# Attention, experts and MLP on one core: score matmuls of two key blocks in the two halves of TensorE's rows, scores computed three steps ahead, gate and float64 splits moved into the expert stage

## The chip, the core and the metric

The program runs on one core of a Trainium2 chip, as one launch. The metric is the device time in microseconds (us). TensorE (PE) multiplies, VectorE (DVE) and ScalarE (ACT) do the element-wise work, GpSimd (POOL) does some of it and issues the indirect transfers, SyncE (SP) issues the other transfers. PE writes only to PSUM, which has eight banks of 2 KB in each of 128 partitions.

## The reference

Three layers follow each other on 24,576 tokens (8 batches of 3,072) of width 256:

```python
# attention: z is (8, 3072, 64), u and v are (8, 3072, 256)
attn = np.maximum((1.0 / S) * z @ z.transpose(0, 2, 1), 0.0) ** 2
x = (u * (attn @ v)).reshape(B * S, D)
# mixture of 8 experts, one for each token
logits = normalise(x) @ normalise(expert_emb).T / tau
idx = argmax(logits, axis=1); gate = softmax(logits)[token, idx]
out[mask_e] = gate * (np.maximum(x[mask_e] @ w1[e], 0.0) @ w2[e])   # w1 256x1024, w2 1024x256
# MLP; w_in (256x2048) and w_out (2048x256) arrive as float64
h = out @ w_in; y = (h - np.tanh(h)) @ w_out
```

## The kernel before, in words

Every float32 operand of a matmul is kept as two parts, a rounded high part and the remainder (`split`, line 102), and a product is made of three matmuls: high by high, high by low, low by high.

**Attention.** A batch has 3,072 keys in 24 blocks of 128. The queries are taken 512 at a time (a *query block*; 48 in all, numbered q), and for each of them the keys two blocks at a time: 12 *steps* per query block, 576 in all, numbered G.

`emit_S(G)` (line 486) makes the scores of step G. z has 64 columns, so a transposed tile `zt` holds the high part of z in partitions 0 to 63 and the low part in 64 to 127; `zs` is the same with the halves swapped, made by two DMAs (`z_swap`). One matmul of `zt` by `zt` over all 128 rows gives high by high plus low by low, and one of `zt` by `zs` gives the two mixed products: two matmuls of 512 columns for a key block, four in a step (lines 493, 494), into a two-bank PSUM tile `s`. Then ACT takes relu (line 500) and square (501), ACT or DVE rounds the square to `ah` (502, the choice is `on_act`), and DVE subtracts to get the remainder `al` (503).

`emit_AV(G)` (line 505) multiplies by v: 24 matmuls of 256 columns (lines 519, 520, 521: `ah` by `vh`, `ah` by `vl`, `al` by `vh`) into `acc`, two banks for a query block. The loop at the end of `attention` issues `emit_S(step + 2)`, `emit_AV(step)` and then whatever the table `steps` holds for this step, so scores are two steps ahead, and the ACT and DVE work on them is issued together with them. All engines take their instructions in this order.

After the last step of a query block, `r_x` (537) multiplies `acc` by u on DVE, into rows `xr`. In the steps that follow come the routing: row norms (`r_n`, ACT), 32 products with the expert embeddings (`r_l`, line 555, DVE), softmax and first maximum (`r_s1`, `r_s2`), ranks by a small matmul (`r_pe`, copied out of PSUM by ACT), the gate times the rows (`r_g`, line 266, DVE), positions (`r_s3`) and a scatter to DRAM (`r_sc`, POOL). In the same stage the expert weights are split (`w_split`: ACT, POOL, and back to DRAM), and w_in and w_out are converted from float64 and split (`f64_split`: nine DVE operations at line 590 and three on POOL for each of 16 pieces) and stored in DRAM.

In PSUM, attention has four single-bank accumulators (two query blocks) and two two-bank score tiles, which the transposes of z and the ranks use as well.

**Experts.** 100 tiles of 256 tokens: `gather` (POOL, indirect), `trans` (PE transposes, line 309, and a split), `up` and `down` (three matmuls a product again). Five gather buffers. Six transfers (`w_piece`) bring the split w_in and half of w_out from DRAM.

**MLP.** 512 tokens at a time against all of w_in and w_out, which lie in SBUF; the change touches only where these weights come from.

Of the kernel before, what the change touches and what calls it, by code (L numbers as in the profile page):

```python
# [12 lines left out]
I32 = mybir.dt.int32  # L13
# [11 lines left out]
def tile_attention_moe_mlp(  # L25
# [31 lines left out]
    ROW = D + 1  # L57
# [7 lines left out]
    wsi = dram.tile([P, 2, KD * F2], F32, tag="wsi", name="wsi")  # L65
    wso = dram.tile([P, 2, KF2 * D], F32, tag="wso", name="wso")
# [162 lines left out]
    def r_s1(q):  # L229
# [13 lines left out]
        nc.vector.tensor_tensor(out=oh, in0=w, in1=b3(m8), op=ALU.is_equal)  # L243
        r["ex"] = ex = sm.tile([P, 4, E], F32, tag="ex", name=f"ex{q}")
        nc.scalar.activation(out=ex, in_=lg, func=AF.Exp)

    def r_s2(q):
# [10 lines left out]
        nc.vector.reciprocal(sx, sx)  # L258
        r["gate"] = sx

    def r_g(q):
        r = RT[q]
        for j in range(4):
            sx = r["gate"]
            x = r["xr"][:, j, 0:D]
            nc.vector.tensor_scalar(out=x, in0=x, scalar1=sx[:, j:j + 1], scalar2=None, op0=ALU.mult)

    def r_pe(q):
        r = RT[q]
        rp = ps_s(f"rp{q}", (P, 2, 256))  # L270
        rp = rp[:, 0, 0:4 * E].rearrange("p (j e) -> p j e", j=4)
        nc.tensor.matmul(rp, tri, r["oh"], start=True, stop=False)
        nc.tensor.matmul(rp, ones, r["cp"], start=False, stop=True)
        r["rk"] = rk = sm.tile([P, 4, E], F32, tag="rk", name=f"rk{q}")
        nc.scalar.copy(rk, rp)
# [28 lines left out]

    def trans(t):
        pt = ps_a(f"xt{t}", (P, KD * TT))
# [8 lines left out]
    def attention(L1, R1, RE):  # L315
# [3 lines left out]
        pr = pool(L1, "pr", 2)  # L319
        pa = pool(L1, "pa", 3)  # L320
        pzs = pool(L1, "pzs", 3)
        pzt = pool(L1, "pzt", NCH + 2)
        pvh = pool(L1, "pvh", NPR + 2)
# [3 lines left out]
        pc = pool(R1, "pc", 1, "right")  # L327
# [4 lines left out]
        ZR, ZZ, ZT, ZS, VR, VH, VL = {}, {}, {}, {}, {}, {}, {}  # L332
# [10 lines left out]
        def z_first():  # L343
            zr = ZR.pop((0, 0))
            ZZ[0, 0] = t = pz.tile([P, 4, P], FR, tag="zz", name="zz0_0")
            w = pz.tile([P, 4, P], FR, tag="zw", name="zw", bufs=1)
            split(t[:, :, 0:64], t[:, :, 64:P], zr, copy=nc.vector.tensor_copy)
            split(w[:, :, 64:P], w[:, :, 0:64], zr)
            z_trans(0, 0)
            z_split(0, 1, nc.vector.tensor_copy)  # L350
# [6 lines left out]
        def z_trans(b, c):  # L357
            zz = ZZ.pop((b, c))
            pt = ps_s(f"pt{b}_{c}")
            for j in range(4):  # L360
                nc.tensor.transpose(pt[:, 0, j * P:(j + 1) * P].bitcast(FR), zz[:, j, :], identr)
            ZT[b, c] = t = pzt.tile([P, 512], FR, tag="zt", name=f"zt{b}_{c}")
            nc.scalar.copy(t, pt[:, 0, :])
# [11 lines left out]
        def v_split(b, g, cp=None):  # L375
            VH[b, g] = h = pvh.tile([P, 2, D], FR, tag="vh", name=f"vh{b}_{g}")
            VL[b, g] = l = pvh.tile([P, 2, D], FR, tag="vl", name=f"vl{b}_{g}")
            cp = cp or (nc.vector.tensor_copy if on_act(g - 2) else nc.scalar.copy)
# [102 lines left out]
        AH, AL, ACC = {}, {}, {}  # L481

        def on_act(step):
            return 2 <= step % NPR < 10 or step // NPR == NQ - 1

        def emit_S(G):
            q, g = divmod(G, NPR)
            b, c = divmod(q, NCH)
            sp = ps_s(f"s{G}")
            for i in range(2):  # L490
                kb = 2 * g + i
                zt = ZT[b, kb // 4][:, (kb % 4) * P:(kb % 4 + 1) * P]
                nc.tensor.matmul(sp[:, i, :], zt, ZT[b, c], start=True, stop=False)
                nc.tensor.matmul(sp[:, i, :], zt, ZS[b, c], start=False, stop=True)  # L494
            r = pr.tile([P, 2, 512], F32, tag="r", name=f"r{G}")
            a = pr.tile([P, 2, 512], F32, tag="a", name=f"a{G}")
            AH[G] = h = pa.tile([P, 2, 512], FR, tag="ah", name=f"ah{G}")
            AL[G] = l = pa.tile([P, 2, 512], FR, tag="al", name=f"al{G}")
            for i in (slice(0, 1), slice(1, 2)) if G == 0 else (slice(0, 2),):
# [77 lines left out]
        def idle():  # L577
            pass
# [501 lines left out]
```

## Time and profile before

| what | us |
|---|---|
| median of 3 runs (5693.11 to 5703.36) | 5699.75 |
| profiled execution, device time | 5693.57 |
| its span | 5692.0 |
| attention, from the start to the last product with v (2296.6) | 2297 |
| experts, to the last product of `down` (3503.5) | 1207 |
| MLP, to the end | 2188 |

Over the span PE is busy 5600.8 us (98%), DVE 4597.2 (81%), ACT 3704.8 (65%), POOL 2054.1 (36%). A matmul's busy time runs from its first column to its last result, so that the bars of matmuls that follow each other overlap; the spacing of their starts tells what one costs. PEld is the loading of a matmul's stationary operand; it is shown apart, and a wait of a matmul often stands there. A wait that ends at an engine which is not the bottleneck costs nothing by itself. The granted clock of TensorE is 0.998 of full speed over the run, that is its higher level, 2.4 GHz.

### The profile page before, as it was taken

Reading aid. Unit: us, or ns where it says so; the run is one execution under the profiler, and the core shown is the slowest. Engines: PE = TensorE matmul, PEld = TensorE weight load, DVE = VectorE, ACT = ScalarE, POOL = GpSimd, SP = SyncE. Lnnn points to the kernel's source line nnn. Section 1 sums busy time; section 2 is a strip of 40 time slices with the busy share of each in tenths; the row PEclk is TensorE's granted clock in tenths of the full one; section 3 lists DMA queues with packets and bytes.
Section 4 is the critical chain, followed back from the end, with each engine's and each line's share of the span. In section 5 each row is a group of like instructions: output and inputs, shape, how many; then the busy total and the mean of one; then the engine's idle time right before and its main releaser. Section 6 shows DMA issues by size and latency. Waiting matters only on the chain. (4 is left out here: it accounts for less than half of the span.)

```text
span 5692.0 us, 99647 instructions
## 1 busy us (share of the span) xinstructions
PE 5600.8 (98%) x38768; PEld 5202.0 (91%) x38768; DVE 4597.2 (81%) x7691; ACT 3704.8 (65%) x4509; POOL 2054.1 (36%) x1381
## 2 busy tenths in 40 slices
PE   9999999999999999999999999999999999999999
PEld 9999999999999999999999998999999999999998
DVE  7989988888989887633333335999999999999999
ACT  8778777777777777322222224777777777777776
POOL 2323232222322221322222221555555555555554
PEclk9999999999999999999999999999999999999999
DMA  2222222222222111344443441000000000000000
GB/s 77 89 73 86 69 87 76 83 72 82 79 80 75 58 41 40 86 117 106 103 105 103 117 127 53 23 23 23 26 26 24 24 23 23 23 28 24 25 23 19
DMA packets 178733, 347.44 MB, mean 61 GB/s; under 512 B 49745, under 2 KB 90194, under 8 KB 173010
## 3 DMA queue, kind: packets, MB, share of 16 engines
q1 hardware_dynamic: 147026, 264.14, 15.9%
q0 software_dynamic: 31232, 76.89, 4.4%
q8 instruction: 307, 5.03, 0.4%
q14 instruction: 168, 1.38, 0.1%
HBM read 520.29 MB, written 118.69 MB: 112 GB/s over the span
## 5 line engine op out<-in xcount | busy, mean ns | idle before, releaser
L521 PE MATMUL acc<-vh,al 128*128 128x256 f32 x4608 | 1308.6, 284 | 38.3 <-DVE al L503 35.2
L519 PE MATMUL acc<-vh,ah 128*128 128x256 f32 x4608 | 1302.3, 283 | 4.3 <-DVE ah L502 4.3
L520 PE MATMUL acc<-vl,ah 128*128 128x256 f32 x4608 | 1302.2, 283 | 0.0
L104 POOL TENSOR_TENSOR gl<-gg,gh 128x1024 fp32r<-128x1024 f32 x381 | 915.1, 2402 | 1009.9 <-ACT gh L103 1003.5
L521 PEld LDWEIGHTS acc<-vh,al 128*128 128x128 f32 x4608 | 879.8, 191 | 51.0 <-DVE al L503 51.0
L519 PEld LDWEIGHTS acc<-vh,ah 128*128 128x128 f32 x4608 | 878.4, 191 | 31.8 <-DVE ah L502 8.6
L520 PEld LDWEIGHTS acc<-vl,ah 128*128 128x128 f32 x4608 | 879.9, 191 | 25.1
L503 DVE TENSOR_TENSOR al<-a,ah 128x1024 fp32r<-128x1024 f32 (+1 forms) x577 | 757.8, 1313 | 141.9 <-ACT ah L502 122.7
L995 PE MATMUL mo<-wo,gl 128*128 128x256 f32 x3072 | 869.5, 283 | 0.0
L993 PE MATMUL mo<-wo,gh 128*128 128x256 f32 x3072 | 868.5, 283 | 0.0
L994 PE MATMUL mo<-wo,gh 128*128 128x256 f32 x3072 | 866.8, 282 | 0.0
L957 ACT ACTIVATE ga<-mh 128x1024 f32<-128x1024 f32 x384 | 395.2, 1029 | 547.2 <-PE mh L955 542.7
L555 DVE CUSTOM_DVE_ANT_0 jl<-xr,en 128x256 f32<-128x256 f32 x1504 | 711.0, 473 | 39.1
L965 DVE TENSOR_SCALAR gm<-ga 128x1024 int32<-128x1024 f32 x384 | 733.2, 1909 | 0.0
L500 ACT ACTIVATE r<-s 128x1024 f32<-128x1024 f32 (+1 forms) x577 | 588.8, 1021 | 216.1 <-PE s L494 211.2
L501 ACT ACTIVATE a<-r 128x1024 f32<-128x1024 f32 (+1 forms) x577 | 611.6, 1060 | 18.3
L953 PE MATMUL mh<-yh,wi 128*128 128x512 f32 (+1 forms) x1568 | 610.4, 389 | 7.9 <-DVE gg L963 6.2
L955 PE MATMUL mh<-yh,wi 128*128 128x512 f32 (+1 forms) x1568 | 611.3, 390 | 0.0
L954 PE MATMUL mh<-yl,wi 128*128 128x512 f32 (+1 forms) x1568 | 610.3, 389 | 0.0
L814 PE MATMUL y<-hh,w 128*128 128x512 f32 x1600 | 581.0, 405 | 18.0 <-DMA w<-ws 15.6
L993 PEld LDWEIGHTS mo<-wo,gh 128*128 128x128 f32 x3072 | 583.6, 190 | 16.4
L994 PEld LDWEIGHTS mo<-wo,gh 128*128 128x128 f32 x3072 | 583.8, 190 | 15.8
(196 smaller groups left out, 12514.6 us busy)
## 6 DMA issues: line engine op xcount, KB each, us to landing
w<-ws SPq DMA_DIRECT2D x180, 2048.0 KB
ys<-yo SPq DMA_DIRECT2D x100, 256.0 KB
vr<-in_v_dram SPq DMA_DIRECT2D x96, 256.0 KB
u<-in_u_dram SPq DMA_DIRECT2D x48, 512.0 KB
yr<-ys SPq DMA_DIRECT2D x47, 512.0 KB
wr<-in_moe_w_dram SPq DMA_DIRECT2D x64, 256.0 KB
ws<-wh SPq DMA_DIRECT2D x64, 256.0 KB
ws<-wl SPq DMA_DIRECT2D x64, 256.0 KB
```

Of the source, the lines that this page charges most:

```text
L104: (eng or nc.vector).tensor_tensor(out=lo, in0=src, in1=hi.bitcast(F32), op=ALU.subtract)
L501: nc.scalar.activation(out=a[:, i], in_=r[:, i], func=AF.Square)
L503: nc.vector.tensor_tensor(out=l[:, i], in0=a[:, i], in1=h[:, i].bitcast(F32), op=ALU.subtract)
L519: nc.tensor.matmul(o, h[:, i, js], vh[:, i, :], start=first, stop=False, skip_group_check=True)
L520: nc.tensor.matmul(o, h[:, i, js], vl[:, i, :], start=False, stop=False, skip_group_check=True)
L521: nc.tensor.matmul(o, l[:, i, js], vh[:, i, :], start=False, stop=last, skip_group_check=True)
L555: nc.vector.tensor_tensor_reduce(out=jk, in0=r["xr"][:, j, 0:D], in1=en[:, e, :], scale=1.0, scalar=0.0, op0=ALU.mult, op1=ALU.add, accum_ ...
L955: nc.tensor.matmul(pv[:, i, :], wi[:, 1, k, fs], yh[:, k, :], start=False, stop=k == KD - 1)
L965: nc.vector.tensor_scalar(out=m, in0=a, scalar1=THR, scalar2=None, op0=ALU.is_gt)
L993: nc.tensor.matmul(o, h[:, i, js], wo[:, 0, fo, :], start=first, stop=False, skip_group_check=True)
L994: nc.tensor.matmul(o, h[:, i, js], wo[:, 1, fo, :], start=False, stop=False, skip_group_check=True)
L995: nc.tensor.matmul(o, l[:, i, js], wo[:, 0, fo, :], start=False, stop=last, skip_group_check=True)
```

## The change

1. **Scores.** A key block's score is now three matmuls over 64 rows (high by high, high by low, low by high; the product of the two low parts is left out). The first key block of a step uses partitions 0 to 63, the second 64 to 127, in turn, so that two matmuls that follow each other lie in different halves of the rows and write different PSUM banks. `zs` is now needed for the keys too.
2. **Order.** Scores are made for three steps at once (18 matmuls), three steps before they are used. Relu, square and split are no longer issued with them but spread over the following three steps (`cycle`). `r_x` is issued ahead of the other element-wise work of its step.
3. **PSUM.** Three two-bank score tiles and one pair of accumulators instead of two and two. The ranks are read from PSUM by DVE (`r_s3`), without the copy; the transposes of z are copied out a step later (`z_copy`).
4. **Casts.** Of every four `ah`, three are made on ACT and one on DVE (before: by `on_act`, 386 and 191). The v splits alternate between the two.
5. **Gate.** The gate is written as one more column of the scattered row (`ROW = D + 2`), and applied after the gather (`scale`, two DVE operations for a tile) instead of before the scatter.
6. **float64.** The 16 pieces are converted in the expert stage, three parts of a piece for each tile, straight into the MLP's tiles; only the second half of w_out goes through DRAM.
7. `r_l` uses `scalar_tensor_tensor` in place of `tensor_tensor_reduce`.

```diff
+        def emit_S(G):
+            SP[G] = sp = ps_s(f"s{G}")
+            TS = ZT, ZS
+            for ki, qi in ((0, 0), (0, 1), (1, 0)):
+                for i in range(2):
+                    kb = 2 * g + i
+                    h = slice(64 * i, 64 * i + 64)
+                    zk, zq = TS[ki ^ i][b, kb // 4], TS[qi ^ i][b, c]
+                    nc.tensor.matmul(sp[:, i, :], zk[h, (kb % 4) * P:(kb % 4 + 1) * P], zq[h, :],
+                                     start=ki == qi, stop=ki == 1)
+        def emit_R(G, i=slice(0, 2)):
...
+            nc.scalar.activation(out=RS[G][:, i], in_=SP[G][:, i], func=AF.Relu, scale=1.0 / S)
+        def emit_A(G, i=slice(0, 2)):
...
+            nc.scalar.activation(out=a, in_=a, func=AF.Square)
+            split(AH[G][:, i], AL[G][:, i], a, copy=nc.vector.tensor_copy if G % 4 == 3 or G == 0 else None)
...
+        cycle = ["r0 r1 a0", "r2 a1", "a2"]
         for step in range(-2, NG):
-            if step + 2 < NG:
-                emit_S(step + 2)
+            base = step - step % GS + GS
+            scores, after = plan.get(step) or (range(base, base + GS) if step == base - GS else (), cycle[step % GS])
+            for G in scores:
+                if G < NG:
+                    emit_S(G)
             if step >= 0:
                 emit_AV(step)
+            # r_x of this step, then the parts named in `after`, then the rest of the step's table
...
+    def scale(t):
+        for j in range(JT):
+            x = XG[t][:, j, 0:D]
+            nc.vector.tensor_scalar(out=x, in0=x, scalar1=XG[t][:, j, D + 1:D + 2], scalar2=None, op0=ALU.mult)
...
@@ experts: each(t)
-            if t in pieces:
-                w_piece(pieces.index(t))
+            if t > K0 and (parts or todo):
+                bg_step()
+                bg_step()
+                bg_step()
...
-                PS["a"] = pool(L1, "psA", 4, space=PSUM)
-                PS["s"] = pool(L1, "psS", 2, space=PSUM)
+                PS["a"] = pool(L1, "psA", 2, space=PSUM)
+                PS["s"] = pool(L1, "psS", 3, space=PSUM)
```

How the order moves, at three places. First PE at the end of query block 16 and the start of block 17 (`acc16`, `acc17` are their accumulators, `s206` a score tile by its step number, `zt2_5` the tile of batch 2 and key group 5). Before:

```order
L521 MATMUL acc16_1_10218<-vh2_11_7656,al203_10683 128x256
L361 MATMUL pt3_0_10825<-identr_75,zz3_0_10712 128x128 x4
L493 MATMUL s206_10849<-zt2_5_7654,zt2_1_7173 128x512
L494 MATMUL s206_10849<-zs2_5_9634,zt2_1_7173 128x512
L493 MATMUL s206_10849<-zt2_5_7654,zt2_1_7173 128x512
L494 MATMUL s206_10849<-zs2_5_9634,zt2_1_7173 128x512
L519 MATMUL acc17_0_10862<-vh2_0_6983,ah204_10736 128x256
```

The same place now, up to the second of three score tiles:

```order
L533 MATMUL acc16_1_10205<-vh2_11_7823,al203_10631 128x256
L501 MATMUL s207_10812<-zt2_5_7589,zt2_1_7150 128x512
L501 MATMUL s207_10812<-zs2_5_7591,zs2_1_7152 128x512
L501 MATMUL s207_10812<-zs2_5_7591,zt2_1_7150 128x512
L501 MATMUL s207_10812<-zt2_5_7589,zs2_1_7152 128x512 x2
L501 MATMUL s207_10812<-zs2_5_7591,zt2_1_7150 128x512
L501 MATMUL s208_10819<-zt2_5_7589,zt2_2_7345 128x512
L501 MATMUL s208_10819<-zs2_5_7591,zs2_2_7347 128x512
```

Steps 207, 208 and 209 now stand together, 18 score matmuls, between the last product into `acc16` and the first into `acc17` (which is now the same pair of banks); where one step's four stood, and none stands before the next two steps.

Second DVE at the same place; `xr16` is `r_x` of block 16, which reads the accumulators. Before:

```order
L502 CAST ah205_10795<-a205_10794 128x1024
L503 TENSOR_TENSOR al205_10796<-a205_10794,ah205_10795 128x1024
L104 TENSOR_TENSOR zz3_1_10832<-zr3_1_10653,zz3_1_10832 128x4x64
L537 TENSOR_TENSOR xr16_10841<-acc16_0_10217,u16_10258 128x2x256
L537 TENSOR_TENSOR xr16_10841<-acc16_1_10218,u16_10258 128x2x256
L502 CAST ah206_10856<-a206_10855 128x1024
L503 TENSOR_TENSOR al206_10857<-a206_10855,ah206_10856 128x1024
L266 TENSOR_SCALAR xr15_10196<-xr15_10196,sx15_10780 128x256 x4
```

Third DVE a little later, in the third step of the next block, now (`rp16` is the tile of the ranks in PSUM, `jl17` the scratch of `r_l`):

```order
L103 TENSOR_TENSOR al220_11630<-a220_11580,ah220_11629 128x1024
L567 SCALAR_TENSOR_TENSOR jl17_0_0_11641,lg17_11592<-xr17_11508,en_157 128x256
L567 SCALAR_TENSOR_TENSOR jl17_0_1_11643,lg17_11592<-xr17_11508,en_157 128x256
L567 SCALAR_TENSOR_TENSOR jl17_0_2_11645,lg17_11592<-xr17_11508,en_157 128x256
L567 SCALAR_TENSOR_TENSOR jl17_0_3_11647,lg17_11592<-xr17_11508,en_157 128x256
L103 TENSOR_TENSOR al221_11674<-a221_11627,ah221_11673 128x1024
L278 TENSOR_TENSOR t16_11678<-rp16_11634,ecap_86 128x32
L279 TENSOR_TENSOR t16_11678<-t16_11678,oh16_11443 128x32
```

The row with `rp16` frees a score tile's place in PSUM and stands behind the remainder `al221` of the last of the three steps; before, ACT's copy of the ranks freed it in the step in which they were made, and the multiplication by the gate (line 266) is gone from this queue.

## Rows read from the trace of the kernel before

**Rows 1.** Busy time by stretch: start, end, its length, each engine's busy time

```profile
0.00:20.00 20.00, 14.50 (x86) 12.60 (x87) 13.42 (x29) 13.36 (x19) 5.73 (x12) 1.00 0.49 151
20.00:2290.00 2270.00, 2219.04 (x16282) 2098.66 (x16281) 1984.22 (x5283) 1772.27 (x2196) 606.06 (x489) 1.00 0.22 72
2290.00:3490.00 1200.00, 1182.03 (x8413) 1106.83 (x8412) 441.49 (x790) 348.28 (x611) 286.66 (x308) 0.99 0.41 105
3490.00:5692.00 2202.00, 2185.25 (x13992) 1983.87 (x13990) 2158.02 (x1591) 1570.92 (x1686) 1155.61 (x573) 1.00 0.08 25
```

**Rows 2.** Waits of PE's weight loads, 0 to 2290: total, times, longest

```profile
PEld acc L521 <- DVE al L503: 51.0, 63, 2.0
...
PEld s L493 <- ACT r L500: 11.3, 14, 1.8
...
PEld acc L519 <- DVE ah L502: 8.6, 10, 1.1
```

**Rows 3.** Timeline of PE, one step: start, duration, line

```profile
1002.97 0.40 PE L493 MATMUL s<-zt,zt 128*128 128x512 f32 x1
...
1003.90 0.28 PE L519 MATMUL acc<-vh,ah 128*128 128x256 f32 x1
1004.02 0.28 PE L520 MATMUL acc<-vl,ah 128*128 128x256 f32 x1
...
1006.76 0.40 PE L493 MATMUL s<-zt,zt 128*128 128x512 f32 x1
```

**Rows 4.** Timeline around one wait for a remainder; brackets: idle before, releaser

```profile
2008.69 0.28 PE L519 MATMUL acc<-vh,ah 128*128 128x256 f32 x1
2008.69 0.19 PEld L520 LDWEIGHTS acc<-vl,ah 128*128 128x128 f32 x1
...
2009.22 0.19 PEld L521 LDWEIGHTS acc<-vh,al 128*128 128x128 f32 x1 [0.34 <-DVE al L503]
2009.22 0.39 PE L521 MATMUL acc<-vh,al 128*128 128x256 f32 x1
```

**Rows 5.** ACT's groups, 0 to 2290: count, busy, mean ns, idle before

```profile
L501 ACT ACTIVATE a<-r 128x1024 f32<-128x1024 f32 x575 | 610.4, 1062 | 18.2
L500 ACT ACTIVATE r<-s 128x1024 f32<-128x1024 f32 x575 | 587.7, 1022 | 214.8 <-PE s L494 209.8 <-issue 2.4
L502 ACT CAST ah<-a 128x1024 fp32r<-128x1024 f32 x386 | 406.2, 1052 | 12.2
L548 ACT ACTIVATE jk<-xr 128x256 f32<-128x256 f32 x188 | 78.1, 415 | 35.6 <-DVE xr L537 32.7
...
L548 ACT ACTIVATION_READ_ACCUMULATOR jk<-xr 128x1 f32 x188 | 35.2, 187 | 0.0
```

**Rows 6.** DVE's groups, 0 to 2290

```profile
L503 DVE TENSOR_TENSOR al<-a,ah 128x1024 fp32r<-128x1024 f32 x574 | 755.2, 1316 | 141.5 <-ACT ah L502 122.4 <-DVE ah L502 1.4 <-issue 0.8
L555 DVE CUSTOM_DVE_ANT_0 jl<-xr,en 128x256 f32<-128x256 f32 x1504 | 711.0, 473 | 39.1
...
L502 DVE CAST ah<-a 128x1024 fp32r<-128x1024 f32 x189 | 129.7, 686 | 81.3 <-ACT a L501 76.4 <-PE acc L521 4.9
...
L266 DVE TENSOR_SCALAR xr<-xr,sx 128x256 f32<-128x256 f32 x184 | 85.7, 527 | 0.0
L537 DVE TENSOR_TENSOR xr<-acc,u 128x512 f32<-128x512 f32 x94 | 60.2, 683 | 0.0
...
L590 DVE TENSOR_SCALAR qe<-qr 128x512 int32<-128x512 int32 x32 | 13.5, 421 | 0.0
...
L590 DVE SCALAR_TENSOR_TENSOR qm<-qe,qp 128x512 f32<-128x512 int32 x16 | 11.0, 687 | 0.0
```

**Rows 7.** Waits in the expert stage, 2290 to 3490

```profile
POOL xg L300 <- PE xt L309: 692.3, 86, 10.6
...
PE y L814 <- DMA w<-ws: 15.6, 9, 4.2
```

**Rows 8.** One line's instructions: the products with `al`, first and last start

```profile
L521 PE MATMUL acc<-vh,al x4608: 277/283/436, 12.8 to 2296.6; 128*128 128x256 f32 x192
```

More of the change, by code (lines that the diff above doesn't have):

```diff
@@ L257, in r_s2 @@
         nc.vector.tensor_scalar(out=sx, in0=sx, scalar1=1e-9, scalar2=None, op0=ALU.add)
[L258 to L266, printed above, removed]
+        nc.vector.reciprocal(r["xr"][:, :, D + 1:D + 2], sx[:, :, None])
     def r_pe(q):
@@ L488, in emit_S @@
             b, c = divmod(q, NCH)
[L489 to L499, printed above, removed]
-                nc.scalar.activation(out=r[:, i], in_=sp[:, i], func=AF.Relu, scale=1.0 / S)
-                nc.scalar.activation(out=a[:, i], in_=r[:, i], func=AF.Square)
-                (nc.scalar.copy if on_act(G - 2) else nc.vector.tensor_copy)(h[:, i], a[:, i])
-                nc.vector.tensor_tensor(out=l[:, i], in0=a[:, i], in1=h[:, i].bitcast(F32), op=ALU.subtract)
+            SP[G] = sp = ps_s(f"s{G}")
[8 more added lines that the diff above has]
+        def emit_R(G, i=slice(0, 2)):
+            if G not in RS:
+                RS[G] = pr.tile([P, 2, 512], F32, tag="a", name=f"a{G}")
+            nc.scalar.activation(out=RS[G][:, i], in_=SP[G][:, i], func=AF.Relu, scale=1.0 / S)
+        def emit_A(G, i=slice(0, 2)):
+            if G not in AH:
+                AH[G] = pa.tile([P, 2, 512], FR, tag="ah", name=f"ah{G}")
+                AL[G] = pa.tile([P, 2, 512], FR, tag="al", name=f"al{G}")
+            a = RS[G][:, i]
+            nc.scalar.activation(out=a, in_=a, func=AF.Square)
+            split(AH[G][:, i], AL[G][:, i], a, copy=nc.vector.tensor_copy if G % 4 == 3 or G == 0 else None)
         def emit_AV(G):
@@ L554, in r_l @@
                 jk = pj.tile([P, D], F32, tag="junk2", name=f"jl{q}_{e}_{j}")
[L555 to L557 removed]
+                nc.vector.scalar_tensor_tensor(
+                    out=jk, in0=r["xr"][:, j, 0:D], scalar=1.0, in1=en[:, e, :],
+                    op0=ALU.mult, op1=ALU.mult, accum_out=r["lg"][:, j, e:e + 1])
         bg = []
@@ new lines, in jobs @@
+        def jobs():
+            a = w_out.bitcast(I32).rearrange("(k p) f -> p k f", p=P)
+            kk = CW // D
+            half = KF2 // 2 // kk
+            WO0 = WO[0].rearrange("p a k f -> p a (k f)")
+            for k in [*range(half, 2 * half), *range(half)]:
+                yield a[:, k * kk:(k + 1) * kk, :], wso if k >= half else WO0, k % half * CW
+            a = w_in.bitcast(I32).rearrange("(k p) f -> p k f", p=P)
+            WI0 = WI[0].rearrange("p a k f -> p a (k f)")
+            for k in range(KD):
+                for f in range(F2 // CW):
+                    yield a[:, k:k + 1, 2 * f * CW:2 * (f + 1) * CW], WI0, k * F2 + f * CW
@@ L779, in weights, with bg_step @@
+        todo, parts = list(jobs()), []
+        def bg_step():
+            if not parts and todo:
+                parts.extend(f64_split(*todo.pop(0), len(todo)))
+            if parts:
+                parts.pop(0)()
         def weights(t, W, ws):
@@ L855, in run @@
             tokens(t0 + 1)
+            scale(t0 + 2)
             each(-1)
@@ L882, in each @@
                 y_load(1)
-        pieces = [NT0 - 8 - max(1, NT0 // 24) * i for i in range(6)][::-1]
         run(0, NT0, each)
+        assert not parts and not todo
         if NT0 < NT:
```

259 lines of the change are left out of this document (130 added, 129 removed).

## The prediction

> **What bounds the kernel now.** I read the busy time by stretch first. PE is busy 2219 of 2270 us in attention, 1182 of 1200 in the experts, 2185 of 2202 in the MLP [rows 1]: the end is set by PE throughout, and a change pays by what it takes from PE's stream or from its waits. The MLP keeps its instructions, so attention and experts are left.
>
> Next the timeline of PE, for the price of a matmul by spacing. One step is 1002.97 to 1006.76, 3.79 us: four score matmuls in 0.93 us (0.2325 each), then 24 products with v in 2.86 us (0.119 each) [rows 3]. 576 steps of 3.79 are 2183 us, and the stage's last product starts at 2296.6 [rows 8].
>
> Then PE's waits. Most are for the remainder `al`, 51.0 us in 63 waits; for `ah` 8.6; and 11.3 before the scores, for the relu that frees a score tile [rows 2]. That is 71 us, in a stage where DVE works 1998 us and ACT 1786 of 2290 [rows 1]: neither is full, they are late.
>
> **Scores.** Before, 4 matmuls a step, 12 in three steps: 12 x 0.2325 = 2.79 us. Now 18 matmuls of 512 columns over 64 rows, in nine pairs in different halves. No row shows two halves working at once. The bounds: a pair costs what one matmul costs (9 x 0.2325 = 2.09 us), or the halves take turns (18 x 0.2325 = 4.19). I take 2.09: the columns of a pair go to different rows and different banks, and weights already load while a matmul runs: the load for L520 starts at 2008.69, the instant at which L519 starts [rows 4]. Two loads for a pair must fit into 0.2325; a load that nothing hides lengthens a product by 0.11 (0.39 against 0.28) [rows 3, 4], so two are 0.22, which fits barely. Gain: 0.70 us x 192 triples = 134 us.
>
> **Turning between whole and half rows.** Twice in a triple PE goes from 128-row matmuls to 64-row ones and back. A product's bar is 0.28 us at a spacing of 0.119 [rows 3], so 0.16 us pass between its last column and its last result. If PE runs empty at each turn, that is 2 x 0.16 x 192 = 61 us. Bounds: nothing, or 0.27 a turn (0.16 and an unhidden load of 0.11) and 0.12 once for the second half starting late, 0.66 x 192 = 127 us. I take 61.
>
> The Trainium skill, "TensorEngine Tiling (Array Packing)", section "Key Properties", says that a change of tiling mode drains TensorE; it speaks against this change and prices nothing. No run here shows a turn yet. By that rule the sum holds the 61 us above; without it they would be gone and the time 61 us lower.
>
> **Waits removed.** Relu, square and split of a triple are issued over the three steps before its first product. ACT's work for a triple is 3 x 1.02 + 3 x 1.06 + 2.25 x 1.05 = 8.6 us [rows 5]; the first `al` is ready some 5 us into the triple and wanted 11 us in, at the next triple's products. So the 60 us of waits for `al` and `ah` go. The 11 us before the scores I leave in. Bounds 0 and 71.
>
> Does ACT or DVE become late as a whole? Casts on ACT go from 386 to 432 (+48 us), the v splits add about 11, the copies of ranks go (-9): 1786 + 50 = 1836 us, 9.6 for a triple. DVE loses the float64 work (16 pieces, five operations of 421 and four of about 687 ns, 78 us), the gate (86) and 46 casts of 686 ns (32) [rows 6]: 1998 - 196 = 1802, 9.4. PE's triple is 3 x 2.86 + 2.09 + 0.32 = 11.0 us. Both fit, with little over. I count nothing for `scalar_tensor_tensor` in `r_l`: it would come off an engine that has room (nearest row 473 ns for 256 elements; were it slower by a third, DVE would have 1.2 us more a triple, 10.6, and still fit).
>
> **Waits added.** (a) The ranks hold a score tile until DVE has read them behind `al` of the triple's last step. In the block's first triple ACT starts when the first tile is there (0.16 + 0.70 = 0.9 us), then has 8.3 us (one cast on DVE) and four row norms of 0.6 [rows 5], so it ends at 11.6 us; `al` takes 1.3 [rows 6], 12.9. PE wants that place for the third tile of the next triple at 11.0 + 0.16 + 1.4 = 12.6. Behind that matmul stands PE's whole stream. With half a weight split (0.3) on ACT the wait is some 0.5 us, in 46 blocks 23 us; bounds 0 and 60 (1.3 each). (b) One pair of accumulators: `r_x` (2 x 0.683 us [rows 6]) must end before the next block's products, behind a burst of 2.1 us or more. The first half is needed first, so 1.4 us of cover remain against a DVE operation under way; I count 0.1 x 47 = 5 us, bounds 0 and 0.68 x 47 = 32 (no cover).
>
> **Experts.** DVE gets 200 `scale` operations (527 ns, 106 us) and the 78 us of float64: 441 + 184 = 625 of 1200 us [rows 1, 6], and does not bound. `scale(t + 3)` waits for a gather, and the next tile's split, which PE wants, stands behind it in DVE's queue. But POOL waits 692 us for the transposes that free a gather buffer [rows 7]: gathers already run as far ahead as five buffers allow. On POOL the three float64 operations of a piece wait for DVE and hold the gathers behind them for about one tile of 12 us (1200 us for 100); three tiles of lead cover that. On SP, 16 loads and 8 stores wait likewise and hold the weight loads, for which PE waits 15.6 us now [rows 7]. I take 0, bounds -10 and +16 (the same again). The longer row (two columns) adds nothing to a stream at 22% of the DMA engines [rows 1].
>
> **Sum.** -134 + 61 - 60 + 23 + 5 = -105 us. The profiled execution took 5693.6 us (span 5692.0), so 5589; the median of the runs is 6 us above that execution, so I forecast 5595 us.
>
> **Rivals.**
>
> *Turns are free.* For: no row shows PE emptying between unlike matmuls. Against: a product's result stands 0.16 us behind its last column [rows 3], and what comes out must not mix. The 61 us stay: 5534; with no wait left at all 5495.
>
> *Turns dear, or ACT late.* 127 in place of 61 gives 5661; with the upper ends of (a) and (b), 64 more, 5725. For: ACT has 1.4 us over in a triple, and the first of each block is over (11.6 of 11.0). Against: a later triple of the block is under.
>
> *The halves don't hide their loads (the slower side).* If a half cannot take weights while it multiplies, a pair is 0.2325 + 0.11 = 0.34 us, the burst 3.08 in place of 2.09: +190 us, 5785. If the halves take turns altogether, 4.19: +403, 5998. It decides from 105 / (192 x 9) = 0.06 us more for a pair, that is 0.29. Against: over whole rows the load does run beside a matmul on the same rows [rows 4].
>
> The Trainium skill, "TensorE: Matmul & The Clock Gate", section "Part 3: Packing small matmuls — row/col tiling", says that weight loads overlap matmuls in flight only when the row groups differ. By that rule each pair would show one load and the time would be this rival's 5785. The trace disagrees for whole rows: load and matmul both start at 2008.69 on the same 128 rows [rows 4].
>
> *The change does not do what it says:* the scores gain nothing net (turns at 0.35) and only the waits move, while ACT's lateness gives them back: within 0.2% of now.
>
> **Chances.** About 0.2%, 11 us, is what a measurement of this kernel can tell from no change. Forecast (5555 to 5635) 0.46; free turns 0.20; dear turns or late ACT 0.16, of which 0.02 end past 5711; no net change 0.04; loads that a half doesn't hide 0.09, halves in turn 0.05. So faster 0.46 + 0.20 + 0.14 = 0.80, same 0.04, slower 0.02 + 0.09 + 0.05 = 0.16. From 5500 to 5720 only the best corner of the free turns (0.04) and the slower rivals (0.14 and a little) are left out; the forecast's own range is 5555 to 5635.
>
> **What will show it.** Right: score matmuls of a pair start within 0.12 us of each other and pairs 0.23 apart; a hole of 0.1 to 0.2 us at each turn; waits for `al` and `ah` near zero; a wait of about half a microsecond for `rp`'s reader once in a block; attention near 2190 us; experts and MLP unchanged within 10 us. Wrong: pairs over 0.29 apart, turns over 0.4, PE waiting for ACT's relu in every triple, or PE waiting in the experts for transposed tiles or weights.

## The result, and the profile after

The changed kernel took 5634.61 us (median of 4 runs, 5629.93 to 5646.35) beside 5696.58 us for the kernel before on the same chip: a ratio of 0.9897, interval 0.9881 to 0.9913. It is faster by 62 us; 5595 had been forecast, in a range from 5500 to 5720.

The profiled execution took 5633.72 us, its span 5632.1. Where the stages end shows where the time went. First starts and last starts of three lines: the products with `al` in attention, the first layer of the experts, the first layer of the MLP; the first answers [rows 8]:

```profile
L533 PE MATMUL acc<-vh,al x4608: 274/283/416, 11.8 to 2219.9; 128*128 128x256 f32 x192
L839 PE MATMUL h<-xh,w x1600: 277/280/416, 2221.9 to 3434.6; 128*128 128x256 f32 x178
L995 PE MATMUL mh<-yh,wi x1568: 280/393/472, 3449.8 to 5608.8; 128*128 128x512 f32 x188, 128*128 128x256 f32 x8
```

Attention ends at 2219.9 instead of 2296.6, 76.7 us sooner. The experts, from their first product to the MLP's first, take 1227.9 us; before it was 1208.6 (2296.8 to 3505.4). With a hole of 2.0 us before them, 0.2 before, they give back 21 us. The MLP is 4 us shorter. -76.7 + 21 - 4 = -60, the difference of the spans.

The waits of PE's weight loads in attention answer [rows 2] (total, times, longest):

```profile
PEld acc L531 <- issue: 52.2, 142, 0.7
PEld s L501 <- DVE t L278: 38.9, 41, 2.3
PEld acc L531 <- DVE cp L255: 13.8, 39, 0.4
PEld acc L531 <- DVE xr L549: 10.9, 7, 1.8
```

Of the three waits of before, for `al`, `ah` and the relu, which made 71 us, 0.6 us are left. The first and third row are, by their length, turns back to whole rows (142 and 39 of the 192, some 0.36 us each; VectorE's `cp` had only ended last). New are the second, a score tile that the ranks still hold, and the fourth, the accumulators. A load's idle time is more than the delay of PE, so PE's own waits for the same two tiles follow:

```profile
PE s L501 <- DVE t L278: 26.4, 15, 1.9
PE acc L531 <- DVE xr L549: 8.1, 6, 1.4
```

By the starts on PE's timeline, the 15 waits delay it by 1.0 to 2.1 us each, 29 us in all. The other 26 idle times of loads behind `t` are of 0.2 us and delay a pair by 0.07 (0.30 us instead of 0.23, at 487.45).

One burst of scores on PE's timeline, with the last product before it and the first two behind, answers [rows 3] (start, duration):

```profile
1005.52 0.28 PE L533 MATMUL acc<-vh,al 128*128 128x256 f32 x1
1005.73 0.50 PE L501 MATMUL s<-zt,zt 64*128 64x512 f32 x1
1005.74 0.50 PE L501 MATMUL s<-zs,zs 64*128 64x512 f32 x1
1006.07 0.39 PE L501 MATMUL s<-zs,zt 64*128 64x512 f32 x1
...
1006.53 0.39 PE L501 MATMUL s<-zt,zt 64*128 64x512 f32 x1
1006.54 0.39 PE L501 MATMUL s<-zs,zs 64*128 64x512 f32 x1
1006.77 0.39 PE L501 MATMUL s<-zs,zt 64*128 64x512 f32 x1
...
1007.68 0.39 PE L501 MATMUL s<-zs,zt 64*128 64x512 f32 x1
1008.00 0.38 PE L531 MATMUL acc<-vh,ah 128*128 128x256 f32 x1
1008.22 0.28 PE L532 MATMUL acc<-vl,ah 128*128 128x256 f32 x1
```

The two matmuls of a pair start 0.01 us apart, the pairs 0.23 apart: the halves work at once, at the price of one matmul. A turn is to be read from what is missing at the usual spacings (0.12 between products). Into the halves: 1005.73 instead of 1005.64, and the first pair takes 0.34 (1005.73 to 1006.07) instead of 0.23, together 0.20. Back: 1008.00 instead of 1007.91, and 0.22 to the next product instead of 0.12, together 0.19. Each turn is a hole of 0.09 us and a weight load that nothing hides. The burst is 9 x 0.23 + 0.39 = 2.46 us; before, the same scores took 2.79.

Two stretches of 20 us (busy time of PE, its loads, DVE, ACT, POOL, then the granted clock): the second batch ends in the first (the next block's products start at 571.78), and the second follows it. PE's wait there comes from its timeline:

```profile
560.00:580.00 20.00, 18.67 (x156) 17.77 (x155) 19.27 (x40) 17.07 (x26) 7.50 (x8) 1.00 0.41 128
580.00:600.00 20.00, 18.08 (x133) 15.91 (x132) 15.60 (x51) 12.50 (x14) 5.19 (x5) 0.91 0.09 31
```

```profile
584.30 0.49 PE L501 MATMUL s<-zt,zt 64*128 64x512 f32 x1 [1.92 <-DVE t L278]
```

PE waits 1.92 us, and the mean clock of that stretch is 0.91: part of it ran at 1.2 GHz (the products stand 0.21 us apart until 588.15), and (1 - 0.91) x 20 = 1.8 us were lost. Summed over all stretches of attention this is 13.2 us, 5.4 in the kernel before. It does not go with every such wait. Of the thirteen idle times of 2.2 to 2.4 us that the loads have behind `t`, six go with such a stretch; five of these six stand 12.5 us behind an idle time of 1.8 us for the accumulators.

The expert stage answers [rows 7]:

```profile
POOL ids L866 <- DMA ids<-xg: 358.0, 57, 11.3
POOL wi L787 <- DVE qyl L760: 84.7, 7, 22.3
POOL qyh L787 <- DVE qyl L760: 65.8, 4, 26.6
POOL wo L787 <- DVE qyl L760: 52.7, 4, 21.9
POOL xg L298 <- PE xt L312: 90.3, 14, 8.7
...
PE y L854 <- DMA w<-ws: 20.9, 5, 5.8
...
PE h L839 <- DMA w<-ws: 7.7, 4, 3.8
```

POOL's gathers are held by the transposes for 90 us, before for 692: they no longer run as far ahead as the buffers allow. The three rows at L787 are the waits of the float64 operations for VectorE, 203 us in 15 times. The first row is POOL waiting for a gather to land; before, that made 67.4 us in 21 times. PE waits 28.6 us for weights instead of 15.6. The gathers' queue in this stage (packets, MB, share of 16 DMA engines), after:

```profile
q0 software_dynamic: 12800, 26.54, 23.0%
```

and before, for the same bytes:

```profile
q0 software_dynamic: 12818, 26.45, 9.1%
```

### The profile page after: what moved, and what is told of

It is laid out like the page before. It is cut to its first block, busy times and chain, and to the rows that moved or that the text cites. A ratio compares the mean times of both kernels' runs of the same rounds, so it can differ in the third digit from the quotient of the medians.

```text
span 5632.1 us, 102164 instructions
## 1 busy us (share of the span) xinstructions
PE 5536.1 (98%) x39920; PEld 5100.3 (91%) x39920; DVE 4509.2 (80%) x7637; ACT 3670.5 (65%) x4525; POOL 2063.5 (37%) x1381
## 5 line engine op out<-in xcount | busy, mean ns | idle before, releaser
L531 PE MATMUL acc<-vh,ah 128*128 128x256 f32 x4608 | 1333.6, 289 | 8.1 <-DVE xr L549 8.1
L103 DVE TENSOR_TENSOR al<-a,ah 128x1024 fp32r<-128x1024 f32 (+1 forms) x577 | 704.0, 1221 | 268.4 <-ACT ah L102 191.4
L507 ACT ACTIVATE a<-s 128x1024 f32<-128x1024 f32 (+1 forms) x577 | 568.4, 1020 | 370.1 <-PE s L501 363.1
L567 DVE SCALAR_TENSOR_TENSOR jl<-xr,en 128x256 f32<-128x256 f32 x1504 | 727.3, 484 | 39.1
L854 PE MATMUL y<-hh,w 128*128 128x512 f32 x1600 | 583.8, 407 | 24.5 <-DMA w<-ws 20.9
L514 ACT ACTIVATE a<-a 128x1024 f32<-128x1024 f32 (+1 forms) x577 | 601.9, 1051 | 0.2
```

The source lines that it names most:

```text
L103: (eng or nc.vector).tensor_tensor(out=lo, in0=src, in1=hi.bitcast(F32), op=ALU.subtract)
L531: nc.tensor.matmul(o, h[:, i, js], vh[:, i, :], start=first, stop=False, skip_group_check=True)
L567: nc.vector.scalar_tensor_tensor(out=jk, in0=r["xr"][:, j, 0:D], scalar=1.0, in1=en[:, e, :], op0=ALU.mult, op1=ALU.mult, accum_out=r["lg" ...
```

## The experiments

They ran on other chips, where the kernel before takes 5741 to 5744 us (5697 on the first one), so ratios to it are compared, and stages from the traces. full_rows, rank_first, gate_back and no_f64 ran on one chip; after_again, turn_each, f64_attn and f64_attn_rank on a second; before_again, late_ranks and late_ranks_act on a third; no_pool64 on a fourth. A stage comes from one profiled execution of each kernel. A table of all comes first: when attention's last product starts; the experts from their first product to the MLP's first; the waits of h and of y for `w` there; q0's share there; the ratio with its interval.

| kernel | attention | experts | h, y for w | q0 | ratio |
|---|---|---|---|---|---|
| before, first chip | 2296.6 | 1209 | 0, 15.6 | 9.1% | 1 |
| before_again | 2295.4 | 1262 | 5.2, 43.8 | 10.5% | one run |
| changed, first chip | 2219.9 | 1228 | 7.7, 20.9 | 23.0% | 0.9897 (0.9881-0.9913) |
| after_again | 2221.9 | 1271 | 31.4, 24.1 | 25.3% | 0.9878 (0.9862-0.9895) |
| full_rows | 2255.9 | 1262 | 23.4, 26.3 | 23.3% | 0.9940 (0.9923-0.9956) |
| turn_each | 2338.0 | 1274 | 22.7, 38.3 | 22.9% | 1.0095 (1.0077-1.0112) |
| rank_first | 2207.8 | 1275 | 21.0, 38.3 | 24.4% | 0.9874 (0.9857-0.9890) |
| gate_back | 2230.5 | 1275 | 31.7, 31.1 | 22.2% | 0.9932 (0.9915-0.9950) |
| no_f64 | 2223.8 | 1260 | 6.1, 45.1 | 10.9% | 0.9869 (0.9852-0.9885) |
| no_pool64 | 2220.0 | 1263 | 6.3, 51.2 | 10.3% | 0.9864 (0.9847-0.9881) |
| f64_attn | 2227.2 | 1243 | 4.1, 28.9 | 11.3% | 0.9866 (0.9849-0.9883) |
| f64_attn_rank | 2208.6 | 1267 | 3.8, 52.5 | 11.6% | 0.9843 (0.9827-0.9860) |
| late_ranks | 2200.5 | 1252 | 5.8, 40.1 | 10.2% | 0.9831 (0.9814-0.9847) |
| late_ranks_act | 2197.0 | 1250 | 3.8, 40.6 | 9.9% | 0.9837 (0.9819-0.9854) |

Attention is alike on all chips (2295.4 and 2296.6; 2221.9 and 2219.9). The expert stage isn't.

**after_again and before_again: no edit.**

> The changed kernel unaltered, on the same chip as the three runs beside it, so that stages can be compared without a difference between chips. Theory A (the weight loads of the expert stage depend on the chip: the four earlier runs, on a chip where the kernel before took 5741 us, waited 50 to 63 us for them whatever was left out, and the changed kernel on the first chip 29 us): a ratio to the kernel before within 0.988 to 0.992; on a chip as slow as that one the waits for w are 45 to 60 us and the expert stage is 1245 to 1275 us long, with attention's last product at 2220 to 2226 us. Rival B (the waits were made by the edits): waits for w of 25 to 35 us on any chip.

> The kernel before unaltered, for its trace beside the two others on a chip that may be slower in the expert stage than the first one. Theory A (the slower chips load weights more slowly, whatever the kernel): on a chip where it takes about 5740 us its waits for w are 35 to 50 us (15.6 us on the first chip), its expert stage 1235 to 1250 us (1208.5 us there), as f64_attn's 1243 us, and attention still ends at 2294 to 2300 us. Rival B (the expert stage of the kernel before doesn't depend on the chip): stage 1205 to 1215 us, and the time is lost in attention or the last stage.

PE's waits for weights in the kernel before, on the slower chip:

```profile
PE y L814 <- DMA w<-ws: 43.8, 11, 6.1
...
PE h L799 <- DMA w<-ws: 5.2, 1, 5.2
```

49 us there, 15.6 on the first chip, and a stage of 1262 us: the same program gets its weights later on such a chip, and a few us of the experts can't be compared across chips. (Theory A had 35 to 50 and 1235 to 1250.) after_again waits 55.5 us on such a chip and attention ends at 2221.9, as its theory A had it; the ratio of 0.9878 lies just under its range. Its stage is 9 us longer than before_again's, where 19 us lay between the two on the first chip.

**full_rows: the scores over whole rows, the order as changed.**

```diff
-            for ki, qi in ((0, 0), (0, 1), (1, 0)):
...
-                    nc.tensor.matmul(sp[:, i, :], zk[h, (kb % 4) * P:(kb % 4 + 1) * P], zq[h, :],
-                                     start=ki == qi, stop=ki == 1)
+            for i in range(2):
...
+                nc.tensor.matmul(sp[:, i, :], zt, ZT[b, c], start=True, stop=False)
+                nc.tensor.matmul(sp[:, i, :], zt, ZS[b, c], start=False, stop=True)
```

> The changed kernel with one part undone: the scores again by four matmuls over all 128 rows for a step, three steps at once, everything else as changed. Theory A (scores pay): in the changed kernel's trace a burst of 18 half-row matmuls with both turns takes 2.46 us, twelve whole-row ones take 12 x 0.2325 = 2.79; so the burst grows by 0.33 us, attention by 192 x 0.33 = 63 us to some 2283 us, the total to 5697 us, and no gaps stand at the turns. Rival B (the turns eat all, and the 62 us measured come from the waits for the remainder that went): the total stays within 10 us of 5635.

A burst, with the products before and behind it:

```profile
1012.40 0.28 PE L530 MATMUL acc<-vh,al 128*128 128x256 f32 x1
1012.52 0.40 PE L498 MATMUL s<-zt 128*128 128x512 f32 x1
...
1015.27 0.28 PE L528 MATMUL acc<-vh,ah 128*128 128x256 f32 x1
```

It takes 2.75 us and has no hole at either end: the holes come with the halves. The halves save 2.75 - 2.46 = 0.29 us a triple, 56 us in 192, but attention ends only 34 us later without them (theory A had 63). The rest had come back as waits. Without the halves PE's own waits for `t` are 19.9 us and for `xr` 1.7, with them 26.6 and 9.5 (after_again), and low clock costs 4.0 us instead of 13.0: 56 - 7 - 8 - 9 = 32. Rival B is out. So of the 74 to 77 us that attention gained, 34 are the halves and 40 all the other parts of the change together. That the waits for `al`, `ah` and the relu are gone puts the order of the scores first among these; gate_back and f64_attn below put 9 and 5 us to the gate and the float64 work. No run undoes the order alone.

**turn_each: scores every step (those of step + 4).**

```diff
...
-            scores, after = plan.get(step) or (range(base, base + GS) if step == base - GS else (), cycle[step % GS])
+            scores, after = plan.get(step) or ([step + 4], cycle[step % GS])
```

> Scores are turned to every step (those of step + 4) instead of three at once every third step: some 383 bursts more, and as many turns back. Theory A (each burst costs the two turns that the timeline shows, 0.39 us in all): attention 383 x 0.39 = 150 us longer than after_again's, 140 to 165 us, and the idle PEld time of acc behind issue grows from 52 us to about three times that. Rival B (a good part of the 0.39 us is the length of the last matmuls and is hidden where the burst is short): 40 to 100 us longer. Rival C (the bursts of three also cost ScalarE and VectorE by their lumps): less than 40 us longer.

One burst on PE's timeline, and the row of the turns back among the waits:

```profile
1006.47 0.28 PE L533 MATMUL acc<-vh,al 128*128 128x256 f32 x1
1006.68 0.50 PE L501 MATMUL s<-zt,zt 64*128 64x512 f32 x1
...
1007.57 0.39 PE L531 MATMUL acc<-vh,ah 128*128 128x256 f32 x1
1007.79 0.28 PE L532 MATMUL acc<-vl,ah 128*128 128x256 f32 x1
```

```profile
PEld acc L531 <- issue: 175.2, 481, 0.7
```

1006.59 to 1007.57, and 0.10 behind: 1.08 = 3 x 0.23 + 0.39. The price of a pair of turns is the same for six matmuls in a burst as for 18. Attention grew by 116 us, between theories A and B; 383 x 0.39 is 149. The slower PE no longer waits for `t` (-29), the clock loses 5.8 us instead of 13.0 (-7), and PE waits some 10 us more for the accumulators (9.5 in after_again):

```profile
PE acc L531 <- DVE xr L549: 19.2, 7, 2.8
```

149 - 29 - 7 + 10 = 123, near the 116. A's mechanism stands, its sum had left out the waits given back.

**rank_first: the ranks' read ahead of the square splits of its step.**

```diff
-                if f is r_x:
+                if f in (r_x, r_s3):
                     f(*a)
...
-                if f is not r_x:
+                if f not in (r_x, r_s3):
```

> The changed kernel with one edit: the reading of the ranks from PSUM is issued with r_x, ahead of the step's square and remainder on VectorE. Theory A: PE waits 38.9 us in 41 waits for this read, because it stands behind the last remainder of the triple, and after the longest of them, at batch ends, the granted clock is at half for 3.4 us; with the read ahead the waits fall under 5 us, the half-clock stretches at the batch ends go, attention is 2220 - 39 - 8 = 2173 us and the total 5588 us. Rival B (ScalarE is late as a whole, the read only stood last): the third score tile is then held by its relu, PE waits about as long for ScalarE, and the total stays within 10 us of 5635.

The wait for `t` is gone (39 to 0.4 us), and the accumulators' wait has grown to

```profile
PEld acc L531 <- DVE xr L549: 27.2, 7, 3.9
```

Attention is 14 us shorter, not the 47 of theory A (39 of waits and 8 of clock): at the seven batch ends PE arrives sooner at a DVE that is still late, and the clock loses 18.4 us instead of 13.0. The gain in time (0.9874 to 0.9878) can't be told from none.

**gate_back: the gate before the scatter, rows of 257 words, no `scale`.**

```diff
-    ROW = D + 2
+    ROW = D + 1
...
+            at(d + 3, r_g, q)
...
-        at(NG - 3, scale, 0)
```

> The changed kernel with the gate multiplied before the scatter again (rows of 257 words, no scale operations in the experts), float64 work still in the experts. The expert stage went from 1208 to 1230 us. Theory A (float64 work delays weight loads and gathers): experts stay at 1225 to 1235 us and attention gets 2 to 20 us longer by the gate's 86 us on VectorE; total 5637 to 5655. Rival B (the scale operations or the wider rows are what slows the gathers, whose packets take 217 ns in place of 129): experts come back to 1210 us or less and the packets to about 130 ns; total 5617 to 5635.

The experts are no shorter (1275) without the 200 `scale` operations and the longer row: these didn't lengthen the stage. Attention is 9 us longer, the waits for `t` 45.9 us, and the ratio is 0.9932 instead of 0.9878, with the intervals apart: moving the gate had paid, as theory A has it.

**no_f64 and no_pool64: which arithmetic slows the gathers.** no_f64 leaves out all float64 arithmetic, and two copies on ScalarE write a word of the input in place of the halves; no_pool64 leaves out only GpSimd's three operations a piece:

```diff
-                nc.gpsimd.tensor_tensor(out=h, in0=ff, in1=tl, op=ALU.add)
-                d = ex.bitcast(F32)
-                nc.gpsimd.tensor_tensor(out=d, in0=ff, in1=h.bitcast(F32), op=ALU.subtract)
-                nc.gpsimd.tensor_tensor(out=l, in0=d, in1=tl, op=ALU.add)
+                nc.scalar.copy(h, ff)
+                nc.scalar.copy(l, tl)
```

> The changed kernel without the float64 arithmetic: the pieces are loaded and stored as before, but the nine VectorE and three GpSimd operations of each are left out and ScalarE copies a word instead, so the MLP's weights are not the reference's. Theory A (float64 work is what costs the experts 21 us): experts 1210 us, total 5613. Rival B (scale or the wider rows): experts stay at 1225 to 1235 us, total within 10 us of 5635.

> As the changed kernel, but the last three operations of each of the 16 float64 pieces, which GpSimd does, are left out; two copies on ScalarE write the piece's halves instead (wrong values). VectorE's nine operations for a piece, the loads and the stores stay. It asks which part of the arithmetic makes the gathers' packets slow and the loads of w1 late in the expert stage. Theory A (GpSimd's queue: its operations wait for VectorE's and hold the gathers behind them, so that the gathers fall behind and meet the weight loads): as in no_f64, q0 takes 10 to 12% of the stage, POOL waits 550 to 650 us for the transposes (xg behind xt), the waits of h for w are under 8 us, the stage 1245 to 1265 us, the ratio to the kernel before 0.985 to 0.988. Rival B (VectorE's 78 us of integer operations disturb the gathers): q0 stays at 22 to 25%, the waits of h for w at 20 to 32 us, the stage at 1262 to 1275 us.

Waits of no_pool64 in the stage:

```profile
POOL xg L298 <- PE xt L312: 661.1, 86, 11.4
...
PE y L852 <- DMA w<-ws: 51.2, 8, 10.6
...
PE h L837 <- DMA w<-ws: 6.3, 2, 6.0
```

The 48 float64 operations on POOL are the cause of the late gathers: without them the gathers are again held by the transposes, q0 falls from 25.3% to 10.3%, and `w1` (h) comes in time. no_f64, where VectorE's operations are gone too, shows no more (645.4 us behind the transposes, 10.9%); its stage of 1260 us answers neither of its theories, which had the first chip's figures. In POOL's timeline of after_again one of them stands waiting ahead of the gathers:

```profile
2499.12 1.28 POOL L787 TENSOR_TENSOR qyh<-qyl 128x512 fp32r<-128x512 f32 x1 [18.00 <-DVE qyl L760]
2500.48 1.30 POOL L789 TENSOR_TENSOR qyh<-qyl,qyh 128x512 f32<-128x512 f32 x1
2501.86 1.29 POOL L790 TENSOR_TENSOR qyl<-qyh,qyl 128x512 fp32r<-128x512 f32 x1
2503.30 1.05 POOL L298 DMA_INDIRECT xg<-xs,xi  x1 [0.15 <-issue]
```

POOL stood 18 us for VectorE, with four gathers of 1 us behind it. The 203 us of such waits in the changed kernel and the operations' own 62 (48 x 1.3) are still less than the 692 us that POOL had to spare before. Most of what is left of these goes to gathers that take longer to land. Median time from issue to landing, changed kernel, then no_pool64:

```profile
xg<-xs,xi POOLq DMA_INDIRECT x190, 8.4
```

```profile
xg<-xs,xi POOLq DMA_INDIRECT x190, 3.9
```

But the time hardly follows: the waits for `w2` (y) rise from 24.1 to 51.2 us as those of h fall, 57.5 us for both beside 55.5 in after_again, and the stage is 1263 instead of 1271 us. So these operations are not shown to be what PE waits for.

**f64_attn: the splits back in attention, stores to wsi and wso, six 1 MB loads late in the experts.**

```diff
...
-            if step > NPR and (step // NPR) % NCH != NCH - 1 and step % 3 == 0:
-                bg_step()
+            if step > NPR and (step // NPR) % NCH != NCH - 1:
+                bg_step(f64_split if step % 3 else w_split)
```

> The float64 splits go back to attention, two steps in three, with their stores to wsi and wso and the six 1 MB loads late in the expert stage, as the kernel before has them; all the rest stays as changed. Theory A (the 8 MB of raw weights that the splits load and the 2 MB that they store fall among the weight loads of an expert, when the DMA engines are full, and cost the expert stage 13 to 20 us; attention has room for the arithmetic, 78 us of VectorE): the expert stage 13 to 20 us shorter than after_again's, the waits for w 10 to 18 us less, the share of queue q0 back near 10% of the stage, attention 0 to 8 us longer, in all 8 to 18 us less than after_again. Rival B (the stage grew by the gate's products, the 258-word rows and the earlier end of attention): the stage within 5 us of after_again's. Rival C (VectorE is the engine that is late at batch ends and before each rank): attention 10 to 30 us longer, more waits for t and xr, and no gain in all.

Attention grows by 5 us (waits for `t` 47.2 instead of 39.2), the experts fall from 1271 to 1243, PE's waits for weights there from 55.5 to 33.0. But f64_attn_rank, with the same expert stage on the same chip, has 1267 and 56.3. In four kernels with the splits in attention the stage is 1243, 1267, 1252 and 1250 us (and 1262 in before_again, which has them there too), in the two that have the loads and stores but not GpSimd's operations 1260 and 1263, in the five with all in the experts 1271, 1262, 1275, 1275 and 1274. The means are 1253, 1261 and 1271, but steps of 8 and 10 us are no more than the scatter within a group (24 in the first, 13 in the last), and the chips differ. What the place of the splits costs the stage is not shown. In all, 5664 beside 5678 us on one chip; the intervals overlap.

**f64_attn_rank and late_ranks: both edits, then the ranks two steps later.**

```diff
-            d = e0 + 10
+            d = e0 + (12 if q < NQ - 3 else 10)
```

> As f64_attn, and the ranks' reads of their sums (r_s3) are issued ahead of the square splits of their step, as in rank_first. Theory A: the waits of the scores for t (38.9 us of PEld in the changed kernel) go, attention ends 12 to 18 us sooner than in f64_attn, as it did in rank_first (2207.8 us against 2223.8 us in the run beside it), and the kernel is the fastest of all, a ratio to the kernel before of 0.980 to 0.986. Rival B: with the float64 arithmetic back in attention VectorE has no slack, and what the ranks gain comes back as waits for r_x (acc behind xr) at batch ends: within 6 us of f64_attn.

> f64_attn_rank with the rank group of a query block (r_n3, r_s1, r_ex, r_s2, r_pe, r_s3, r_sc) two steps later, so that it follows the multiply that reads the accumulators (r_x) of the next block instead of preceding it. Theory A (what is left of f64_attn_rank's waits at batch ends, 27.6 us of acc behind xr, 3.5 us each, is VectorE's queue ahead of r_x: r_s1's small operations took 1.1 to 1.2 us each there): these waits fall under 12 us, attention ends 10 to 25 us sooner than f64_attn_rank's 2208.6 us, and the kernel takes 0.977 to 0.983 of the kernel before, the fastest of all. Rival B (VectorE is full in these stretches whatever the order): the wait goes to t, al or ah of the next steps, and attention ends within 6 us of 2208.6 us. Rival C: the ranks later push the scatter of a block and the accumulators of the block after it wait: slower.

The read ahead takes the wait for `t` away here too (47.2 to 0.8 us), attention ends 18.6 us sooner than in f64_attn (theory A: 12 to 18), and the ratio is 0.9843, in its range; the intervals of the two overlap. 27.6 us of waits for `xr` are left. One thing that makes VectorE late at a batch end, DVE and POOL on the timeline of f64_attn_rank:

```profile
1105.86 0.42 DVE L569 SCALAR_TENSOR_TENSOR jl<-xr,en 128x256 f32<-128x256 f32 x1
1106.09 2.78 POOL L104 TENSOR_TENSOR vl<-vr,vh 128x512 fp32r<-128x512 f32 x2 [2.50 <-PE s L503]
...
1106.32 1.39 DVE L569 SCALAR_TENSOR_TENSOR jl<-xr,en 128x256 f32<-128x256 f32 x1
...
1107.76 1.40 DVE L569 SCALAR_TENSOR_TENSOR jl<-xr,en 128x256 f32<-128x256 f32 x1
...
1109.20 0.43 DVE L569 SCALAR_TENSOR_TENSOR jl<-xr,en 128x256 f32<-128x256 f32 x1
```

The same operation takes 0.42 us alone and 1.4 while POOL subtracts two halves of v. The Trainium skill, "Advanced Engine Details and Errata", section "VectorE Performance Modes", says that VectorE's second SBUF port is shared with GpSimd, so that GpSimd instructions and VectorE instructions in a two-port mode block each other. 1.4 instead of 0.42 us beside a GpSimd operation is what such blocking would look like; whether this operation counts among those the page means, no run here shows. With the rank group behind `r_x` the wait for `xr` falls to 20.4 us, not under 12, but low clock costs 6.0 us instead of 16.2 and attention ends at 2200.5, 8 us sooner, between theories A and B. With late_ranks_act, which can't be told from it, late_ranks is the fastest kernel here: 5645.38 us beside 5740.64, 0.9831 (0.9814 to 0.9847), against 0.9878 for the change as it was.

**late_ranks_act: all copies of the v splits on ScalarE.**

```diff
-            cp = cp or (nc.vector.tensor_copy, nc.scalar.copy)[g % 2]
+            cp = cp or nc.scalar.copy
```

> late_ranks, and the copies that split v (0.42 us each on VectorE for every second pair of blocks, none on it here) are all on ScalarE. Theory A (VectorE is late at batch ends and ScalarE has room there): another 2 to 8 us off attention. Rival B (ScalarE, which computes relu, square and three of four copies, is the next to be late): no gain or 2 to 10 us more, with waits for ah or for a.

Attention ends 3.5 us sooner, the time is the same (0.9837): within what can be told.

## Why the prediction was right, and where its sizes were off

The direction and the mechanism held: pairs, turns and the waits that go decide it. The size did not: 62 us of 105, at the upper edge of the band from 5555 to 5635 that the forecast gave itself. Of its own signs, the pairs, the holes at the turns and the end of the waits for `al` and `ah` came as said; attention near 2190 us did not (2219.9), and PE waiting in the experts for weights, a sign of being wrong, did (28.6 us instead of 15.6). The terms, in us:

| term | forecast | measured |
|---|---|---|
| pairs | -134 | 192 x (2.79 - 2.07) = -138 |
| turns | +61 | 192 x 0.39 = +75 |
| waits for `al`, `ah`, relu | -60 | -71 |
| ranks hold a score tile | +23 | +29 (38.9 idle on the loads) |
| accumulators | +5 | +8 (10.9 idle on the loads) |
| low clock in attention | none | 13.2 - 5.4 = +8 |
| experts | 0 (-10 to +16) | +21 |

The first six make -89, and attention came out at -76.7. Longer waits at the transposes of z, mostly at the start (11.4 us on the loads instead of 5.2), are 6 of the 12 us between; the rest isn't accounted for. With the experts and the MLP (-4) this is -60, against -105. Nor do the terms stand alone: full_rows shows that of 134 - 61 = 73 us forecast for pairs and turns, 63 by the bursts' length, only 34 reach the end of attention.

1. **Pairs: right.** "The halves don't hide their loads" is refuted: the loads of both halves start together, and a pair takes 0.23 us. The Trainium skill's rule in "TensorE: Matmul & The Clock Gate", "Part 3: Packing small matmuls — row/col tiling", that loads overlap matmuls in flight only for other row groups, does not hold here; the same part also names a load into a background weight buffer, which the prediction left out and to which this trace could belong. From the timeline of PE's weight loads in the changed kernel:

```profile
1006.31 0.18 PEld L501 LDWEIGHTS s<-zt,zt 64*128 64x128 f32 x1
1006.31 0.18 PEld L501 LDWEIGHTS s<-zs,zs 64*128 64x128 f32 x1
1006.54 0.18 PEld L501 LDWEIGHTS s<-zs,zt 64*128 64x128 f32 x1
```

The last of these loads goes to rows on which the pair of 1006.53 and 1006.54 has just begun (both halves are busy then), and the next pair still follows 0.23 us later.

2. **Turns: right in kind, a fifth too small.** The drain of 0.16 had been read from the tail of a product; measured are 0.09 of hole and 0.10 to 0.11 of exposed load, 0.2 a turn. The Trainium skill's rule ("TensorEngine Tiling (Array Packing)", "Key Properties"), that a change of mode drains TensorE, agrees with this trace: a hole of 0.09 us at each turn, and none in full_rows. The rival of free turns is out (turn_each).

3. **Ranks: the step was sound, the size near by luck.** 0.5 us in 46 blocks had been forecast, 23 us. Measured are 15 delays of 1.0 to 2.1 us, two near each batch end (as at 534.79 and 584.30, with the batch's end at 571.78), where v and z are split as well; in the other blocks there are 26 of 0.07. The working took a block in mid-batch for all: too much for these, and nothing for the batch ends. VectorE isn't busier than forecast (1794 us in attention, 1802 in the working); it is late in a few places.

4. **Low clock: not foreseen.** Waits of before went up to 2.0 us too [rows 2], and cost 5.4 us of clock. Of the 2.3 us waits of the changed kernel six in thirteen go with a stretch at 1.2 GHz, of late_ranks' 2.7 us waits at the batch ends two in seven, of rank_first's 3.9 us waits there all seven. What decides between waits of one length isn't settled.

5. **Experts: the step that failed.** The prediction had POOL's three operations hold the gathers for about a tile of 12 us, and "three tiles of lead cover that", so it took 0, at most +16. The hold is right on average (203 us in 15 waits, 13.5 each, at most 26.6), the lead isn't: it went (692 us held by buffers before, 90 after), and no_pool64 shows that these operations are the cause. PE's waits for weights rose by 13 us on the first chip, and the clock lost 13.8 us in the stage instead of 7.0; these two make 20 of the 21. That the lost lead made them is not shown: with the lead back, on another chip, PE waits as long for weights (no_pool64, 57.5 us beside 55.5). So the cause of the +21 stays open.

## What to carry to other kernels

Two matmuls of 512 columns over half the rows cost here what one over all rows costs, but each turn between whole and half rows costs 0.2 us, so collect as many half-row matmuls behind one turn as PSUM holds: three tiles paid here, one at a time did not. When PE gets faster, a helper engine that was nearly late becomes late at the places of the densest side work, and part of the gain comes back there as waits (22 of 56 us for the halves), some of them with a stretch at the lower clock behind them. An operation that waits in a queue of gathers can take the gathers' lead away, though it is short itself (48 of 1.3 us here): ask what stands behind it, not only how long it runs.

## What had not been expected of the hardware

- The packets of the gathers take 2.5 times as long (23% of the DMA engines instead of 9% for the same 26.5 MB) with GpSimd's 48 operations between the gathers; without these it is 10.3%. Why a packet takes longer then isn't settled: no run separates the delay of a gather from anything else that the operations do to it.
- The same kernel's expert stage takes 1209 us on one chip and 1262 on another, with attention within 1.2 us (one profiled execution of each; by the medians the kernel takes 5741 to 5744 us on four chips and 5697 on the first). Why isn't shown.
